# Linear attention and two gated layers on one core: both heads' numerators and denominators as products of 64 columns, normalised whole, in the first three blocks

## The chip, the cores and the metric

The kernel runs on one core of a Trainium2 chip. The metric is the device time of one execution in microseconds. The core has TensorE (PE, with its weight loads shown apart as PEld), VectorE (DVE), ScalarE (ACT), GpSimd (POOL) and SyncE (SP), whose queue here issues all DMAs. Each engine works off its own instructions in order and waits for the others by semaphores.

## The reference

Linear attention by random features for 4 x 8 heads of 576 tokens and 64 channels, then a gated layer, then a second layer. What the change touches is the end of the attention, `num` and `den`:

```python
q_p, k_p = phi(q_s), phi(k_s)                 # 128 features
kv = einsum('bhsm,bhsd->bhmd', k_p, v)
z = sum(k_p, axis=2)
num = einsum('bhsm,bhmd->bhsd', q_p, kv)
den = einsum('bhsm,bhm->bhs', q_p, z)[..., None] + 1e-06
x = num / den                                 # 2304 tokens x 512
g = x @ w_gate
x = (g / (1 + exp(-g)) * (x @ w_val)) @ w_out # 512 -> 1536 -> 512
h = x @ w_in                                  # 512 -> 2048
out = where(h >= 1, h, where(h <= -1, 0, (h + 1)**2 / 4)) @ w_out2
```

## The kernel before

The 2304 tokens are nine blocks of 256 (`k` = 0 to 8; a batch has 2.25 of them). The channels of a block lie in four pairs of heads (`p` = 0 to 3), and `d = p // 2` names the half of the 512 channels to which a pair belongs. Keys and values of a batch come in nine groups of 128 tokens (`k_group`): load `ki`, squares on ACT (L572), projection on PE (L599), maximum on DVE (L618), exponential on ACT into `ebk` (L626, or a DVE addition L630 and then L633), and products with the values `vi` (L672), which add up kv and z in a bank of PSUM. `kv_evac` copies that bank to `kvr` as f32 for the first three blocks, and to `kvz` in two parts for the others. The constant `NATK = 3` is the number of blocks that use f32 for this.

Queries (`q_group`) go the same way as far as the exponential (`ebq`), are transposed on PE (L757) and copied to `qtn`. Then `num` does one pair of heads of one block, and that is what is changed, for `k < NATK`; it runs 12 times there. For head `a` of the pair it multiplies the 256 columns of `qtn` with a 128 x 128 matrix of `kvr` (`mm_nat`, L810). The result of head 0 has its numerator on partitions 0 to 63 and its denominator, 64 times the same row, on partitions 64 to 127; for head 1 it is the other way about. Block 2 lies across two batches, and each product of it is two, of 64 and of 192 columns. After that:

- the two denominators are evicted to the other half of `rec`, with 1e-6 added, on ACT (L828) or DVE (L830);
- DVE transposes `rec` by squares of 32 into `rect` (L835), takes the reciprocal of one column of each square (L836) and transposes it back, spread over the square (L838);
- the numerators are multiplied by it, each half by itself: on DVE (L843), or copied by ACT (L848) and multiplied whole on POOL (L850).

The result `os` is split into two parts `x1s` (L373, L383, L385), which the first layer's products take (L392 to L394: high by high, high by low, low by high), and stored to `x1d`. `q_done` tells the stream of keys that a half block is through: the fifth to ninth key group of batch 2 are loaded only after the second half of blocks 0 to 2, by the plan.

What stands where in a queue is set when the program is built. A planner (`Planner`) runs all these processes against a table of costs; each engine takes the ready operation of the best priority, and `pick` gives an operation to the engine that would be done with it first. So any other cost or number of operations gives all engines another order. The order then stands in the program, and on the chip the engines only wait for each other. Buffers come from rings (`Get`, `pl.put`); eight banks of PSUM are one of them. A load into a buffer waits until what was in it has been read, and SP issues in order, so that what stands behind such a load waits too.

Of the kernel before, what the change touches and what calls it, by code (L numbers as in the profile page):

```python
# [22 lines left out]
AF = mybir.ActivationFunctionType  # L23
ALU = mybir.AluOpType
AX = mybir.AxisListType
# [3 lines left out]
P = 128  # L29
TB = 256  # L30
# [10 lines left out]
ALT = 1.63  # L41
# [5 lines left out]
NATK = 3  # L47
# [216 lines left out]
def c_act(n, bias=False):  # L264
    return (115 + n) / 1200.0 + (0.05 if bias else 0.0)


def c_dve(n, psum=False, fast=False):
    return (66 + (n / 2 if fast else n)) / 960.0


def c_pool(n):
    return 0.11 + 0.00218 * n
# [7 lines left out]
def performer_moe_kernel(ctx: ExitStack, tc: tile.TileContext, qG, kG, om, ident,  # L281
                         w1, wo1, w2, wo2, out):
    nc = tc.nc
    pl = Planner()
# [4 lines left out]
    def bufs(pool, name, n, shape, dt=F32):  # L289
        return [pool.tile(shape, dt, tag=f"{name}{i}", name=f"{name}{i}") for i in range(n)]  # L290

    def ring(*a):
        return Ring(bufs(*a))
# [6 lines left out]
    bank = ring(psum, "bank", 8, [P, 512])  # L300
# [19 lines left out]
    att = att_cm.__enter__()  # L320
# [30 lines left out]
    kvr = {(b, d): att.tile([P, 2, 2, P], F32, name=f"kvr{b}_{d}") for b in nat_b for d in range(2)}  # L351
    qts0 = ring(att, "qtn", 3, [P, 2, TB])
    xhl = ring(att, "xhl", 2, [P, 2, 256], F32R)
    stat = ring(att, "st", 10, [P, 4, 4])
    rec = ring(att, "rec", 2, [P, TB])
    rect = ring(att, "rect", 1, [P, TB])
    qts = ring(att, "qt", N_QT, [P, 2, 2, TB], F32R)
    kvz = [[att.tile([P, 2, 2, 2, P], F32R, name=f"kvz{b}_{d}") for d in range(2)] for b in range(2)]
    ids = att.tile([P, P], F32, name="ids")
    omr = att.tile([P, 256], F32, name="omr")  # L360
    omh = att.tile([P, 256], F32R, name="omh")
    oml = att.tile([P, 256], F32R, name="oml")
# [2 lines left out]
    def dma(dst, src, nbytes):  # L365
        yield Op("SP", 0.06, lambda: nc.sync.dma_start(dst, src))  # L366
        yield Op("HW", 0.05, None)
        yield Op("DMA", nbytes / 330e3, None)
# [210 lines left out]
    def margin():  # L579
        if moe_on.done and SLACK_A:  # L580
            yield SLACK_A
# [158 lines left out]
    def q_group(k, p, qb):  # L740
# [23 lines left out]
        else:  # L764
# [6 lines left out]
            else:  # L771
# [3 lines left out]
                yield Op("POOL", c_pool(512), lambda: nc.gpsimd.tensor_tensor(out=lv, in0=e, in1=hv.bitcast(F32), op=ALU.subtract))  # L775
                back(ebufs[True], e)
        pl.spawn(num(k, p, q_t), pl.cur.prio - 0.05)

    def num(k, p, q_t):
        d, r = divmod(p, 2)  # L780
        yield x1_have[k]
        xs = x1_tile[k]
        cuts = []
        t0 = k * TB
        while t0 < (k + 1) * TB:
            b = t0 // 576
            t1 = min((b + 1) * 576, (k + 1) * TB)
            cuts.append((b, t0 - k * TB, t1 - k * TB))
            t0 = t1
        if k < NATK:  # L790
            for b in sorted({c[0] for c in cuts}):
                yield kv_ready[b, d]
        else:
            for b in sorted({c[0] for c in cuts}):
                yield kv_split[b, d]
        if (k, d) not in xd:
            xd[k, d] = Ev(), []
            xd[k, d][1].append((yield Get(osb)))
            pl.set(xd[k, d][0])
        yield xd[k, d][0]  # L800
        x = xd[k, d][1][0]
        xr = x[:, r * TB:(r + 1) * TB]
        rc = yield Get(rec)
        pb = yield Get(bank)
        ps = pb.rearrange("p (a t) -> p a t", a=2)

        def mm_nat():
            for a in range(2):
                for b, c0, c1 in cuts:
                    nc.tensor.matmul(ps[:, a, c0:c1], kvr[b, d][:, r, a], q_t[:, a, c0:c1], start=True, stop=True)  # L810

        def mm():
            for a in range(2):
                for b, c0, c1 in cuts:
                    kz = kvz[b % 2][d]
                    for l, h in ((0, 0), (0, 1), (1, 0)):
                        nc.tensor.matmul(ps[:, a, c0:c1], kz[:, l, r, a], q_t[:, h, a, c0:c1],  # L817
                                         start=(l == 0 and h == 0), stop=(l == 1), skip_group_check=True)
        yield from margin()
        if k < NATK:  # L820
            yield Op("PE", 0.86 if len(cuts) == 1 else 0.95, mm_nat)
        else:
            yield Op("PE", 6 * 0.109 if len(cuts) == 1 else 12 * 0.107, mm)
        pl.put(qts if k >= NATK else qts0, q_t)
        half0, half1 = slice(0, 64), slice(64, P)
        for a, (here, there) in enumerate(((half0, half1), (half1, half0))):
            if pl.pick(ACT=c_act(TB), DVE=c_dve(TB)) == "ACT":
                yield Op("ACT", c_act(TB), lambda: nc.scalar.activation(rc[here], ps[there, a], AF.Copy, bias=1e-6))  # L828
            else:
                yield Op("DVE", c_dve(TB), lambda: nc.vector.tensor_scalar(  # L830
                    out=rc[here], in0=ps[there, a], scalar1=1e-6, scalar2=None, op0=ALU.add))
        tt = yield Get(rect)
        st = yield Get(stat)
        rs = st.rearrange("p a b -> p (a b)")[:, 0:TB // 32]
        yield Op("DVE", c_dve(TB), lambda: nc.vector.transpose(out=tt, in_=rc))  # L835
        yield Op("DVE", 0.135, lambda: nc.vector.reciprocal(out=rs, in_=tt.rearrange("p (n c) -> p n c", c=32)[:, :, 0]))  # L836
        pl.put(rect, tt)
        yield Op("DVE", c_dve(TB), lambda: nc.vector.transpose(  # L838
            out=rc.rearrange("p (n c) -> p n c", c=32), in_=rs.unsqueeze(2).to_broadcast([P, TB // 32, 32])))
        pl.put(stat, st)  # L840
        if pl.pick(DVE=2 * c_dve(TB), POOL=c_pool(TB) + 2 * c_act(TB) + ALT) == "DVE":
            for a, here in enumerate((half0, half1)):
                yield Op("DVE", c_dve(TB), lambda: nc.vector.tensor_tensor(  # L843
                    out=xr[here], in0=ps[here, a], in1=rc[here], op=ALU.mult))
            pl.put(bank, pb)
        else:
            for a, here in enumerate((half0, half1)):
                yield Op("ACT", c_act(TB), lambda: nc.scalar.activation(xr[here], ps[here, a], AF.Copy))  # L848
            pl.put(bank, pb)
            yield Op("POOL", c_pool(TB), lambda: nc.gpsimd.tensor_tensor(out=xr, in0=xr, in1=rc, op=ALU.mult))  # L850
        pl.put(rec, rc)
        q_cnt[k, d] = q_cnt.get((k, d), 0) + 1
        if q_cnt[k, d] < 2:
            return
        pl.set(q_done[k, d])
        yield from x1_split(k, d, x)
        yield from dma(half_block(x1d, k, d), x.rearrange("p (n t) -> p n t", n=2), P * 512 * 4)
        pl.put(osb, x)
# [4 lines left out]
    def half_block(t, k, d):  # L863

        return t[k // 2][:, 2 * d:2 * d + 2, (k % 2) * TB:(k % 2 + 1) * TB]

    def x1_split(k, d, x):
        xs = x1_tile[k]
        hi, lo = (xs[:, l, 2 * d:2 * d + 2].rearrange("p k t -> p (k t)") for l in range(2))
        yield from parts(hi, lo, x, 512)  # L870
        x1_cnt[k] = x1_cnt.get(k, 0) + 1
        if x1_cnt[k] == 2:
            pl.set(x1_ready[k])
# [347 lines left out]
    for m, a, order, sets in passes:  # L1221
        for j in order:
            for c in sets:
                n = 2 if m == 1 and j < 4 else 1 if m == 1 else 4 if j < 4 else 2
# [411 lines left out]
```

## Time and profile before

| | us |
|---|---|
| three timed runs, median (lowest, highest) | 993.88 (991.18, 995.39) |
| the profiled execution | 990.77 |
| its span, first to last instruction | 989.0 |
| PE busy | 968.7 |
| DVE busy | 830.2 |
| ACT busy | 573.8 |
| POOL busy | 100.4 |
| mean granted clock of PE, of 1 | 0.997 |

The profiled execution has its own time, 990.77 us; 1.8 us of it lie around the span. Busy times of a stretch are read against its length. A wait is idle time of an engine just ahead of an instruction, put down to whichever other engine or DMA came last. Matmul records overlap, so one takes longer than the time from one to the next. An f32 product is two instructions in the trace.

### The profile page before, as it was taken

To read this page: it belongs to the slowest core of one execution; us is meant where nothing else is said; L and a number is where in the kernel's file an instruction comes from. 1 tells how busy PE (TensorE), PEld (TensorE's weight loads), DVE (VectorE), ACT (ScalarE), POOL (GpSimd) and SP (SyncE) were. 2 spreads that over 40 slices of the span, in tenths; PEclk is the share of its full clock that TensorE was granted. 3 is DMA by queue.
4 is the path that set the end of the run, shared out by engine and by line. 5 is a ranking of instruction groups with operands and counts; after the bars stand their busy time and mean duration, and the time that the engine had idled before them with its cause. 6 is when DMAs were issued, how large, how long until landed. Compare 5 with 4: busy or idle time off the path is not lost.

```text
span 989.0 us, 18507 instructions
## 1 busy us (share of the span) xinstructions
PE 968.7 (98%) x6778; PEld 900.7 (91%) x6778; DVE 830.2 (84%) x1703; ACT 573.8 (58%) x1477; POOL 100.4 (10%) x101
## 2 busy tenths in 40 slices
PE   7899999999999999999999999999999999999998
PEld 6789899999999999999999999999998989999986
DVE  7999888778789999999999999998788678866553
ACT  8998888968654644464645556564555455544331
POOL 0223344733310000000000000000000000000000
PEclk9999999999999999999999999999999999999999
DMA  8755546545386555756575666246233041403022
GB/s 304 233 175 190 173 150 201 173 150 171 107 267 207 176 180 166 242 192 211 181 245 184 196 222 222 72 132 234 79 114 107 1 139 44 129 2 106 1 86 85
DMA packets 90667, 154.50 MB, mean 156 GB/s; under 512 B 8528, under 2 KB 42320, under 8 KB 90576
## 3 DMA queue, kind: packets, MB, share of 16 engines
q1 hardware_dynamic: 90576, 153.32, 47.6%
q8 instruction: 53, 0.87, 0.3%
q14 instruction: 38, 0.31, 0.1%
HBM read 110.30 MB, written 42.99 MB: 155 GB/s over the span
## 4 chain that ended last, share of the span: by engine, by line
PE 73%; DVE 11%; ACT 6%; DMA 5%; issue 3%; SPq 1%; POOL 0%; POOLq 0%; DVEq 0%; ACTq 0%
PE bank L392 22%; PE bank L394 22%; PE bank L393 22%; PE bank L672 2%; PE bank L599 2%; PE bank L817 1%; SPq L366 1%; PE bank L757 1%; DMA ws<-in_w_dram 1%; DMA ki<-in_kG_dram 1%; ACT ebq L626 1%; PE bank L810 1%; DVE wt L414 1%; DVE x1s L385 1%; ACT rec L828 1%
## 5 line engine op out<-in xcount | busy, mean ns | idle before, releaser
L392 PE MATMUL bank<-x1s,w 128*128 128x256 f32 x492 | 140.1, 285 | 2.7 <-ACT ebk L626 1.9
L394 PE MATMUL bank<-x1s,w 128*128 128x256 f32 x492 | 137.7, 280 | 0.0
L393 PE MATMUL bank<-x1s,w 128*128 128x256 f32 x492 | 137.6, 280 | 0.0
L392 PEld LDWEIGHTS bank<-x1s,w 128*128 128x128 f32 x492 | 92.7, 188 | 7.6 <-ACT ebk L626 2.3
L393 PEld LDWEIGHTS bank<-x1s,w 128*128 128x128 f32 x492 | 92.7, 188 | 3.8
L394 PEld LDWEIGHTS bank<-x1s,w 128*128 128x128 f32 x492 | 92.6, 188 | 0.0
L373 ACT ACTIVATE x1s<-xq 128x512 fp32r<-128x512 f32 x83 | 52.0, 628 | 51.3 <-PE bank L394 33.2
L392 PE MATMUL bank<-x1s,wb 128*128 128x256 f32 x286 | 80.1, 280 | 0.6 <-ACT eb L373 0.6
L394 PE MATMUL bank<-x1s,wb 128*128 128x256 f32 x286 | 79.9, 279 | 0.0
L393 PE MATMUL bank<-x1s,wb 128*128 128x256 f32 x286 | 79.9, 279 | 0.0
L392 PE MATMUL bank<-x1s,wx 128*128 128x256 f32 x278 | 78.7, 283 | 0.1
L394 PE MATMUL bank<-x1s,wx 128*128 128x256 f32 x278 | 78.4, 282 | 0.3 <-POOL wx L383 0.3
L393 PE MATMUL bank<-x1s,wx 128*128 128x256 f32 x278 | 78.4, 282 | 0.0
L373 ACT ACTIVATE eb<-bank 128x512 f32<-128x512 f32 x93 | 55.0, 592 | 28.7 <-PE bank L394 28.1
L385 DVE TENSOR_TENSOR x1s<-xq,x1s 128x512 fp32r<-128x512 f32 x90 | 61.5, 684 | 6.0 <-ACT x1s L373 5.9
L409 ACT ACTIVATE wt<-ws 128x512 f32<-128x512 f32 x68 | 45.7, 674 | 29.3 <-DMA ws<-in_wo_dram 14.9
L392 PEld LDWEIGHTS bank<-x1s,wb 128*128 128x128 f32 x286 | 54.0, 189 | 5.2 <-ACT eb L373 0.8
L393 PEld LDWEIGHTS bank<-x1s,wb 128*128 128x128 f32 x286 | 53.8, 188 | 4.3
L392 PEld LDWEIGHTS bank<-x1s,wx 128*128 128x128 f32 x278 | 52.6, 189 | 3.8 <-ACT eb L373 0.3
L393 PEld LDWEIGHTS bank<-x1s,wx 128*128 128x128 f32 x278 | 52.7, 190 | 3.3
L1251 DVE TENSOR_TENSOR gb<-bank,eb 128x512 f32<-128x512 f32 x64 | 43.8, 685 | 13.4 <-PE bank L394 13.2
L373 ACT ACTIVATE hlr<-hb 128x512 fp32r<-128x512 f32 x51 | 32.1, 630 | 38.7 <-PE bank L393 32.2
(267 smaller groups left out, 3205.7 us busy)
## 6 DMA issues: line engine op xcount, KB each, us to landing
ws<-in_w_dram SPq DMA_DIRECT2D x40, 512.0 KB, 4.9
ws<-in_wo_dram SPq DMA_DIRECT2D x28, 512.0 KB, 4.5
xq<-x1d SPq DMA_DIRECT2D x36, 256.0 KB, 5.0
xq<-x2d SPq DMA_DIRECT2D x36, 256.0 KB, 4.1
qi<-in_qG_dram SPq DMA_DIRECT2D x34, 256.0 KB, 3.1
ki<-in_kG_dram SPq DMA_DIRECT2D x33, 256.0 KB, 4.2
vi<-in_kG_dram SPq DMA_DIRECT2D x28, 192.0 KB, 3.3
x1d<-os SPq DMA_DIRECT2D x18, 256.0 KB, 3.7
```

Source lines behind the costliest of these rows:

```text
L366: yield Op("SP", 0.06, lambda: nc.sync.dma_start(dst, src))
L373: yield Op("ACT", c_act(n), lambda: nc.scalar.activation(dst, src, AF.Copy, scale=1.0 if scale is None else scale))
L385: yield Op("DVE", c_dve(n), lambda: nc.vector.tensor_tensor(out=dst, in0=a, in1=b, op=op), True)
L392: nc.tensor.matmul(ps, l_hi, r_hi, start=first, stop=False, skip_group_check=shared)
L393: nc.tensor.matmul(ps, l_hi, r_lo, start=False, stop=False, skip_group_check=shared)
L394: nc.tensor.matmul(ps, l_lo, r_hi, start=False, stop=last, skip_group_check=shared)
L409: yield Op("ACT", 0.575, lambda: nc.scalar.activation(t, hw.bitcast(F32), AF.Abs))
L414: yield Op("DVE", c_dve(512), lambda: nc.vector.scalar_tensor_tensor(out=ti, in0=lw, scalar=29, in1=ti, op0=ALU.logical_shift_right, op1=A ...
L599: nc.tensor.matmul(ps[:, t * 256:(t + 1) * 256], xt[:, t * P:(t + 1) * P], omr, start=True, stop=True)
L626: nc.scalar.activation(e[:, u * P:(u + 1) * P], ps[:, u * P:(u + 1) * P], AF.Exp, bias=st[:, u, 3:4])
L672: nc.tensor.matmul(kp[:, 2 * pr + a], e[:, u * P:(u + 1) * P], vb[:, vi + (dv if li == 4 else 0), a * 64:a * 64 + P], start=(li == 0 and a ...
L1251: yield Op("DVE", c_dve(512), lambda: nc.vector.tensor_tensor(out=dst, in0=pq(ps), in1=pq(e), op=ALU.add))
```

## The change

For blocks 0 to 2, each head's numerator and denominator are two products of 64 columns of `kvr`. Both numerators go to the same columns of PSUM (`ps[:, 0]`), head 0 on partitions 0 to 63 and head 1 on 64 to 127, and both denominators to `ps[:, 1]` in the same places. So denominators lie where their numerators lie, and the eviction to the other half falls away: DVE transposes the denominators right out of PSUM. `rect` gets a 33rd column for each square that holds 1e-6, and a reduction adds it to the denominator. The product with the reciprocal, or the copy for POOL, is one of 128 partitions instead of two of 64. The other six blocks do what they did (`norm_halves` has the old code). The plan's cost of `mm_nat` is left as it was.

```diff
-    rect = ring(att, "rect", 1, [P, TB])
+    rect = ring(att, "rect", 1, [P, TB // 32, 33])
+    nc.gpsimd.memset(rect.free[0][0][:, :, 32:33], 1e-6)
...
+    halves = slice(0, 64), slice(64, P)
+
+    def norm_whole(ps, pb, rc, xr):
+
+        tt = yield Get(rect)
+        st = yield Get(stat)
+        s8 = st.rearrange("p a b -> p (a b)")
+        yield Op("DVE", 0.36, lambda: nc.vector.transpose(out=tt[:, :, 0:32], in_=ps[:, 1].rearrange("p (n c) -> p n c", c=32)))
+        yield Op("DVE", 0.09, lambda: nc.vector.tensor_reduce(out=s8[:, 0:8], in_=tt[:, :, 0:33:32], axis=AX.X, op=ALU.add))
+        pl.put(rect, tt)
+        yield Op("DVE", 0.135, lambda: nc.vector.reciprocal(out=s8[:, 8:16], in_=s8[:, 0:8]))
+        yield Op("DVE", c_dve(TB), lambda: nc.vector.transpose(
+            out=rc.rearrange("p (n c) -> p n c", c=32), in_=s8[:, 8:16].unsqueeze(2).to_broadcast([P, TB // 32, 32])))
+        pl.put(stat, st)
+        if pl.pick(DVE=c_dve(TB), POOL=c_pool(TB) + c_act(TB) + ALT) == "DVE":
+            yield Op("DVE", c_dve(TB), lambda: nc.vector.tensor_tensor(out=xr, in0=ps[:, 0], in1=rc, op=ALU.mult))
+            pl.put(bank, pb)
+        else:
+            yield Op("ACT", c_act(TB), lambda: nc.scalar.activation(xr, ps[:, 0], AF.Copy))
+            pl.put(bank, pb)
+            yield Op("POOL", c_pool(TB), lambda: nc.gpsimd.tensor_tensor(out=xr, in0=xr, in1=rc, op=ALU.mult))
...
         def mm_nat():
-            for a in range(2):
+            for what in range(2):
                 for b, c0, c1 in cuts:
-                    nc.tensor.matmul(ps[:, a, c0:c1], kvr[b, d][:, r, a], q_t[:, a, c0:c1], start=True, stop=True)
+                    for a in range(2):
+                        nc.tensor.matmul(ps[halves[a], what, c0:c1], kvr[b, d][:, r, a, halves[a ^ what]], q_t[:, a, c0:c1],
+                                         start=True, stop=True, skip_group_check=True)
...
+        if k < NATK:
+            yield from norm_whole(ps, pb, rc, xr)
         else:
...
+            yield from norm_halves(ps, pb, rc, xr)
```

Since the plan is made anew, the order of all engines differs from about the first unit of `num` on. Two places. The first is on ACT, around the seventh exponential of queries (into `ebq_125`), for which PE's transposition at 44.31 us waits. `L828` (after: gone here) evicts a denominator, `L848` and `L798` copy numerators, `L572` and `L573` are squares. Before:

```order
L626 ACTIVATE ebq_126<-bank_67,st_158 128x128 x4
L373 ACTIVATE x1s_103<-os_111 128x512
L828 ACTIVATE rec_167<-bank_64 64x256
L828 ACTIVATE rec_166<-bank_69 64x256
L575 ACTIVATE qi_135<-qi_135 128x256
L572 ACTIVATE ki_127,st_163<-ki_127 128x64 x4
L373 ACTIVATE qtn_151<-bank_67 128x512
L572 ACTIVATE ki_128,st_157<-ki_128 128x64 x4
L848 ACTIVATE os_113<-bank_64 64x256
L633 ACTIVATE ebq_125<-ebq_125 128x512
L848 ACTIVATE os_113<-bank_64 64x256
```

The same place on ACT after:

```order
L374 ACTIVATE qtn_151<-bank_70 128x512
L627 ACTIVATE ebk_121<-bank_63,st_160 128x128 x4
L634 ACTIVATE ebk_124<-ebk_124 128x512
L573 ACTIVATE ki_127,st_163<-ki_127 128x64 x4
L573 ACTIVATE ki_128,st_165<-ki_128 128x64 x4
L798 ACTIVATE os_112<-bank_67 128x256
L576 ACTIVATE qi_135<-qi_135 128x256
L576 ACTIVATE ki_129<-ki_129 128x256
L410 ACTIVATE wt_83<-ws_81 128x512
L798 ACTIVATE os_112<-bank_64 128x256
L627 ACTIVATE ebq_125<-bank_68,st_164 128x128 x4
```

The evictions are gone, each copy is one instead of two, and two exponentials of keys (`ebk_121`, `ebk_124`) have moved ahead of this one of queries.

The second place is on PE, where batch 2's fifth key group is projected (`ki_128`, then `ki_129` and `ki_127`). The rows that are left out repeat the three products above them. Before:

```order
L672 MATMUL bank_65<-vi_130,ebk_123 128x128 x6
L392 MATMUL bank_64<-x1s_104,w_78 128x256
L393 MATMUL bank_64<-x1s_104,w_78 128x256
L394 MATMUL bank_64<-x1s_104,w_78 128x256
...
L672 MATMUL bank_65<-vi_131,ebk_124 128x128 x4
L599 MATMUL bank_67<-omr,ki_128 128x256 x2
```

After:

```order
L673 MATMUL bank_64<-vi_130,ebk_123 128x128 x2
L393 MATMUL bank_63<-hl_109,w_75 128x256
L394 MATMUL bank_63<-hl_109,w_75 128x256
L395 MATMUL bank_63<-hl_109,w_75 128x256
L673 MATMUL bank_64<-vi_131,ebk_124 128x128 x2
...
L395 MATMUL bank_65<-x1s_104,w_78 128x256
L600 MATMUL bank_67<-omr,ki_128 128x256 x2
```

Between the last read of `vi_130` and the projection stood 12 products of the layer and one row of `vi_131`; now 42 products of the layers and two rows of `vi_131` stand there. On SP the order at this place is the same in both: the load of `vi_130`, then the loads of `ki_128`, `ki_129` and `ki_127`.

## Rows read from the trace of the kernel before

**Rows 1.** Page, part 1: busy us (share of the span) and instructions of each engine.

```profile
PE 968.7 (98%) x6778; PEld 900.7 (91%) x6778; DVE 830.2 (84%) x1703; ACT 573.8 (58%) x1477; POOL 100.4 (10%) x101
```

**Rows 2.** Stretches: us, busy of each engine (instructions), granted clock, DMA share, GB/s.

```profile
30.00:40.00 10.00, 9.45 (x59) 8.36 (x59) 9.24 (x29) 9.86 (x38) 3.85 (x4) 1.00 0.83 271
40.00:50.00 10.00, 7.01 (x27) 4.81 (x25) 8.58 (x29) 9.29 (x46) 3.43 (x4) 0.83 0.63 194
50.00:60.00 10.00, 9.11 (x63) 8.35 (x64) 9.68 (x31) 9.93 (x40) 3.28 (x3) 1.00 0.55 165
...
100.00:110.00 10.00, 7.97 (x61) 7.29 (x60) 8.75 (x20) 7.55 (x28) 4.46 (x3) 0.98 0.68 200
110.00:120.00 10.00, 9.67 (x61) 8.76 (x60) 7.59 (x21) 8.17 (x38) 2.07 (x2) 0.85 0.60 206
...
sum 40.00, PE 36.95 PEld 36.14 DVE 32.40 ACT 36.23 POOL 20.91; mean PE 9.24 PEld 9.03 DVE 8.10 ACT 9.06 POOL 5.23
...
200.00:300.00 100.00, 99.98 (x854) 99.78 (x853) 81.22 (x173) 63.23 (x173) 29.74 (x27) 1.00 0.52 172
```

**Rows 3.** PE in order of time, 38 to 47 us: start, length, instructions, idle before.

```profile
38.46 1.13 PE L810 MATMUL bank<-qtn,kvr 128*128 128x256 f32 x4 [0.55 <-ACT kvr L373]
...
42.33 1.13 PE L599 MATMUL bank<-omr,qi 128*128 128x256 f32 x4 [1.43 <-DVE ebq L630]
44.31 0.67 PE L757 MATMUL bank<-ids,ebq 128*128 128x128 f32 x4 [0.86 <-ACT ebq L633]
44.80 1.92 PE L599 MATMUL bank<-omr,qi 128*128 128x256 f32 x4
```

**Rows 4.** ACT in order of time, 43 to 44.3 us.

```profile
43.37 0.37 ACT L848 ACTIVATE os<-bank 64x256 f32<-64x256 f32 x1
43.64 0.62 ACT L633 ACTIVATE ebq<-ebq 128x512 f32<-128x512 f32 x1
```

**Rows 5.** PE in order of time, 101 to 113 us.

```profile
101.47 2.39 PE L672 MATMUL bank<-vi,ebk 128*128 128x128 f32 x20
...
104.36 0.28 PE L394 MATMUL bank<-x1s,w 128*128 128x256 f32 x1
...
105.17 1.05 PE L672 MATMUL bank<-vi,ebk 128*128 128x128 f32 x8
108.15 4.64 PE L599 MATMUL bank<-omr,ki 128*128 128x256 f32 x12 [1.92 <-DMA ki<-in_kG_dram]
```

**Rows 6.** SP's queue in order of time, 102 to 106 us.

```profile
102.55 1.22 SPq L366 DMA_DIRECT2D vi<-in_kG_dram  x2
103.83 1.37 SPq L366 DMA_DIRECT2D ki<-in_kG_dram  x3
```

**Rows 7.** ACT's groups by form, 25 to 110 us: busy us, mean ns, idle before.

```profile
L828 ACT ACTIVATE rec<-bank 64x256 f32<-64x256 f32 x17 | 6.2, 377 | 0.9 <-PE bank L810 0.5
L848 ACT ACTIVATE os<-bank 64x256 f32<-64x256 f32 x10 | 3.7, 374 | 0.1
L575 ACT ACTIVATE ki<-ki 128x256 f32<-128x256 f32 x5 | 2.1, 428 | 0.0
```

**Rows 8.** PE in order of time at 36 us; PEld's group of L810, 0 to 200 us.

```profile
36.02 1.03 PE L599 MATMUL bank<-omr,ki 128*128 128x256 f32 x4
36.89 1.03 PE L810 MATMUL bank<-qtn,kvr 128*128 128x256 f32 x4
...
L810 PEld LDWEIGHTS bank<-qtn,kvr 128*128 128x128 f32 x64 | 10.7, 201 | 2.2 <-ACT kvr L373 1.0 <-ACT qtn L373 0.4
```

**Rows 9.** DVE's groups by form, 25 to 110 us.

```profile
L621 DVE TENSOR_REDUCE st<-st 128x4 f32<-128x8 f32 x53 | 6.5, 146 | 0.2
L843 DVE TENSOR_TENSOR os<-bank,rec 64x256 f32<-64x256 f32 x14 | 5.8, 411 | 0.2
L835 DVE STREAM_TRANSPOSE rect<-rec 128x256 f32<-128x256 f32 x12 | 5.1, 429 | 0.1
L830 DVE TENSOR_SCALAR rec<-bank 64x256 f32<-64x256 f32 x7 | 2.8, 417 | 1.2 <-ACT rec L828 1.0
```

More of the change, by code (lines that the diff above doesn't have):

```diff
@@ new lines, in norm_halves @@
+    def norm_halves(ps, pb, rc, xr):
+        for a, (here, there) in enumerate(((halves[0], halves[1]), (halves[1], halves[0]))):
+            if pl.pick(ACT=c_act(TB), DVE=c_dve(TB)) == "ACT":
+                yield Op("ACT", c_act(TB), lambda: nc.scalar.activation(rc[here], ps[there, a], AF.Copy, bias=1e-6))
+            else:
+                yield Op("DVE", c_dve(TB), lambda: nc.vector.tensor_scalar(
+                    out=rc[here], in0=ps[there, a], scalar1=1e-6, scalar2=None, op0=ALU.add))
+        tt = yield Get(rect)
+        st = yield Get(stat)
+        rs = st.rearrange("p a b -> p (a b)")[:, 0:TB // 32]
+        yield Op("DVE", c_dve(TB), lambda: nc.vector.transpose(out=tt[:, :, 0:32], in_=rc.rearrange("p (n c) -> p n c", c=32)))
+        yield Op("DVE", 0.135, lambda: nc.vector.reciprocal(out=rs, in_=tt[:, :, 0]))
+        pl.put(rect, tt)
+        yield Op("DVE", c_dve(TB), lambda: nc.vector.transpose(
+            out=rc.rearrange("p (n c) -> p n c", c=32), in_=rs.unsqueeze(2).to_broadcast([P, TB // 32, 32])))
+        pl.put(stat, st)
+        if pl.pick(DVE=2 * c_dve(TB), POOL=c_pool(TB) + 2 * c_act(TB) + ALT) == "DVE":
+            for a, here in enumerate((halves[0], halves[1])):
+                yield Op("DVE", c_dve(TB), lambda: nc.vector.tensor_tensor(
+                    out=xr[here], in0=ps[here, a], in1=rc[here], op=ALU.mult))
+            pl.put(bank, pb)
+        else:
+            for a, here in enumerate((halves[0], halves[1])):
+                yield Op("ACT", c_act(TB), lambda: nc.scalar.activation(xr[here], ps[here, a], AF.Copy))
+            pl.put(bank, pb)
+            yield Op("POOL", c_pool(TB), lambda: nc.gpsimd.tensor_tensor(out=xr, in0=xr, in1=rc, op=ALU.mult))
@@ L824, in num @@
         pl.put(qts if k >= NATK else qts0, q_t)
[L825 to L845, printed above, removed]
-        else:
[L847 to L850, printed above, removed]
+        if k < NATK:
+            yield from norm_whole(ps, pb, rc, xr)
+        else:
+            yield from norm_halves(ps, pb, rc, xr)
         pl.put(rec, rc)
```

## The prediction

> **What bounds the kernel now.** I read the busy times of the page first, then the stretches of 10 us, then in the stretches with idle TensorE its own order of time, and behind each of its waits the engine that was waited for. The page has PE busy for 968.7 of 989.0 us [rows 1]. The stretches say where the other 20 us are: from 200 us on PE is full (99.98 of 100 us in the stretch shown), so the change cannot save anything there, it can only disturb. The idle time lies ahead of that, and the three blocks that the change touches are worked on between 27 and 105 us. In 30 to 60 us PE is idle for 0.55 + 2.99 + 0.89 = 4.43 us, and in the middle one of these stretches the granted clock has a mean of 0.83; in 100 to 120 us it is idle for 2.03 + 0.33 = 2.36 us, with clocks of 0.98 and 0.85; in 150 to 190 us for 40.00 - 36.95 = 3.05 us [rows 2].
>
> The first idle stretch is made by ACT and DVE, which are busy for 9.86 + 9.29 + 9.93 = 29.1 us and 27.5 us of these 30 [rows 2]. PE waits 1.43 us until DVE's addition ebq L630 and 0.86 us until ACT's exponential ebq L633 [rows 3]. That exponential stands on ACT right behind a copy of a half (os L848 [rows 4]), and the order shows two evictions of denominators (rec L828) and the next half's copy around it. After those two waits four instructions at 44.80 take 1.92 us where the same four take 1.03 us elsewhere [rows 3, 8]: PE had been idle, and the granted clock then stood at 1.2 of 2.4 GHz. Time lost by it: 10 us x 0.17 = 1.7 us.
>
> The second one is a DMA: PE waits 1.92 us for ki at 108.15, and then twelve instructions take 4.64 us, again at half the clock; (0.02 + 0.15) x 10 = 1.7 us are lost by that [rows 2, 5]. Those loads were issued at 103.83, right behind two loads of vi in SP's queue [rows 6]. The second of these (into vi_130) may not start before PE has read the old vi_130, with the last twelve of the twenty instructions that start at 101.47 and last 2.39 us [rows 5].
>
> **The change, part by part.** *DVE and ACT.* In each of the 12 units (3 blocks x 4 pairs of heads; "unit" below) two evictions of 64 x 256 fall away, 17 on ACT of 377 ns and 7 on DVE of 417 ns, together 9.3 us; and two half products (or half copies) become one whole of the same 256 columns, which saves 12 instructions of 374 to 411 ns, 4.7 us [rows 7, 9]. That a whole one costs what a half does: 128x256 on ACT takes 428 ns, 64x256 takes 374 to 377 [rows 7]. Added is one small reduction for each unit, nearest row 146 ns, 1.8 us in all [rows 9]. The transpose now reads PSUM and writes at a pitch of 33; the nearest row is its old form with 429 ns, and the row of a product that reads 256 columns from PSUM has 411 [rows 9]. I take 0.43 and no change; if the pitch doubled it, that would be 12 x 0.43 = 5.2 us more on DVE, less than what is taken off. Net: 12.2 us less on the two engines, about 7 of the 12 units before 60 us, so 7 us out of that stretch's 56.6.
>
> *PE's first idle stretch.* The order shows what this moves. On ACT, two evictions and the half copies no longer stand ahead of the exponential of ebq_125. I added up the work that the orders put ahead of each transposition on ACT and on PE, each instruction by what rows of its kind take (an estimate): before, ACT's sum is ahead of PE's by 1.8, 3.2 and 2.0 us for the three transpositions around 42 us, so PE must wait; in the new order ACT's is less than PE's by 1.6 to 5.9 us from the fifth to the fourteenth, so PE need not. I count the idle 4.43 us as gone but for the 0.55 us for kvr at 38.46, which has the same neighbours in the new order [rows 3]; and as PE does not idle, the 1.7 us of slow clock go with it. -5.6 us.
>
> *PE's second one.* In SP's queue the loads of ki still stand behind vi_130. But between the last read of the old vi_130 and the first use of ki, PE's new order has 42 products of 0.117 us (104.36 to 105.17 for seven) and 4 of 0.22 us: 5.8 us; before, there were 12 and 4, 2.3 us [rows 5]. From their issue to their first use the loads took 103.83 to 108.15, 4.3 us [rows 5, 6]. So 3.5 us of cover are added where 1.92 were missing: the wait goes, and the slow clock behind it. -3.6 us. What is late next there is nothing that I can name from the rows; the idle 0.33 us and 0.1 us are left.
>
> *PE's third one.* Which waits of 150 to 190 us survive a new order I can't tell: ACT is ahead by more at nearly all places there. Between nothing and 3.05 us I take half, -1.5 us.
>
> *PE's own work.* A unit was 2 products of 256 columns in f32, 4 instructions, 0.87 us (36.02 to 36.89 for four such [rows 8]). Now it is 4 products of 64 output columns, 8 instructions, that still pass all 256 columns each. The trace has no product that fills half the array, so this is bounded: if two products on different halves run side by side all the time, 0.87 us, nothing added; if one after another, 8 x 0.216 = 1.73 us, 12 x 0.86 = 10.4 us more. The code alternates the halves, but each product is two instructions in a row on the same half; if only neighbours on different halves pair, 8 instructions take 5 slots of 0.216, 1.08 us. I take this value, 12 x 0.21 = +2.5 us: it is nearest to the lower end, because PE's rows show that it takes up an instruction before the last is through (a record of 1.03 us for four that come every 0.87 [rows 8]), but it is the least certain term here. After 60 us nothing hides it.
>
> The Trainium skill (TensorEngine Tiling (Array Packing), Key Properties) says that tiles operate independently and can load and multiply in parallel; no run here shows that yet. By it alone the term would be between 0 and +2.5 us. The same section says that a change of the tiling mode drains the engine; there are 24 such changes, and no row prices one.
>
> *Sum.* 990.8 us (989.0 of span and 1.8 around it) - 5.6 - 3.6 - 1.5 + 2.5 = 982.6 us. The profiled run was the fastest seen: the median of the three timed ones is 993.9 and they spread over 4.2 us. Against the median the same difference of -8.2 us gives 985.7; I forecast 986.
>
> **The rivals.** *One after another.* The halves don't pair: +10.4 instead of +2.5. The idle time still goes, since a slower PE waits less: 993.9 - 10.7 + 10.4 = 993.6, no change that can be told. For it: no row of the trace shows two products side by side. Against it: the halves lie on different partitions and are written in turn. Chance 0.25.
>
> *Weights in the open* (slower than before). Each of the 8 instructions of a unit loads its 64 columns, and the load can't hide behind a product that uses the same rows of the array. The price from the rows: at least the pace of 128-column instructions, 0.11 us (105.17 to 106.03 for eight [rows 5]), at most the record of a load, 0.20 us [rows 8]. With 0.11 a unit is 8 x 0.326 = 2.6 us, +20.9 us in all: 993.9 - 10.7 + 20.9 = 1004. It decides from 0.87 + 10.7/12 = 1.76 us a unit, and by more than 0.5% from 2.17. Against it: now the loads do hide, as four instructions with loads of 0.20 us come every 0.87 us. Chance 0.10.
> The Trainium skill (TensorE: Matmul & The Clock Gate, Part 3) has the rule that a load overlaps products in flight only when the row group differs, and here both halves use all rows. The trace disagrees for whole-array products, whose loads overlap.
>
> *The holes move.* All queues are planned anew, and PE's idle time comes back elsewhere ahead of 200 us, with its slow clock: 993.9 + 2.5 = 996.4 at worst, 992 if half of it does. For it: the three holes of before have three different causes. Against it: the sums on ACT above are better everywhere. Chance 0.15.
>
> **How the numbers follow.** The forecast has 0.50. Within it the third idle stretch (0 to 3) and the pairing (0 to 2.5) leave 982 to 990. A measurement of this kernel can tell 0.5%, 5 us, from no change. Faster by more: most of the forecast's 0.50 and a few lucky cases of the others, 0.48. Within 0.5%: the rest of the forecast, one after another, most of the moved holes, 0.38. Slower: the weights in the open and the worst of the holes, 0.14. The range goes from 980 (all holes gone, full pairing) to 997 (holes come back).
>
> **What would show it.** Right: PE busy for nearly all of 30 to 60 us, no granted clock below 1 there or in 100 to 120 us, no wait for ki near 105; units of 1.1 us in PE's order of time. Wrong: a unit of 1.7 us or more, with PE full and the span unchanged; or PE's waits for ebq, ki or a bank back under other names. The forecast fails first at the unit's price on PE.

## The result and the profile after

The kernel after takes 984.08 us (median of four runs, 983.49 to 984.53), the kernel before 994.63 in the same comparison (991.18 to 995.78): ratio 0.9896, with a 95% interval of 0.9874 to 0.9917. 986.0 was forecast. The profiled execution of after took 984.11 us with a span of 982.1; that of before had 990.77 and 989.0.

Page, part 1, of the kernel after: busy us (share of the span) and instructions. [rows 1] answers to it.

```profile
PE 966.7 (98%) x6842; PEld 895.3 (91%) x6842; DVE 825.7 (84%) x1697; ACT 567.3 (58%) x1459; POOL 107.7 (11%) x110
```

The stretches of the kernel after; the columns are those of [rows 2]: us, then busy time of PE, PEld, DVE, ACT and POOL with their instructions, granted clock, DMA share, GB/s.

```profile
30.00:40.00 10.00, 10.00 (x74) 8.39 (x73) 9.57 (x32) 9.90 (x38) 5.23 (x5) 1.00 0.91 288
40.00:50.00 10.00, 10.00 (x72) 8.13 (x71) 9.19 (x38) 8.72 (x41) 4.69 (x5) 1.00 0.87 283
50.00:60.00 10.00, 9.72 (x69) 7.53 (x69) 8.46 (x29) 8.00 (x35) 2.12 (x3) 1.00 0.40 108
100.00:110.00 10.00, 8.74 (x57) 7.68 (x55) 8.49 (x25) 8.25 (x40) 2.64 (x2) 1.00 0.71 236
110.00:120.00 10.00, 9.97 (x86) 9.97 (x87) 8.33 (x20) 8.38 (x22) 5.62 (x6) 1.00 0.42 127
150.00:190.00 40.00, 40.00 (x345) 40.00 (x344) 34.95 (x90) 37.19 (x156) 28.67 (x31) 1.00 0.63 197
300.00:500.00 200.00, 197.40 (x1431) 185.38 (x1430) 190.03 (x365) 105.66 (x196) 0.00 (x0) 1.00 0.61 199
...
980.00:982.00 2.00, 0.00 (x0) 0.00 (x0) 0.00 (x0) 0.00 (x0) 0.00 (x0) 0.77 0.13 44
```

Of the first two holes that the prediction named, that of 30 to 60 us is closed but for 0.28 us; in 100 to 120 us 1.29 of 2.36 us are left, behind other waits. No clock below 1 is left in either. The idle time of PE, from such rows over the whole span, in both profiled executions and in a second one of before that was taken later (last of the experiments):

| stretch, us | idle before | idle before, second profile | idle after |
|---|---|---|---|
| 0 to 20 | 5.38 | 4.78 | 5.24 |
| 30 to 60 | 4.43 | 4.86 | 0.28 |
| 60 to 100 | 0.25 | 0.26 | 0 |
| 100 to 120 | 2.36 | 3.80 | 1.29 |
| 120 to 200 | 3.05 | 3.18 | 0.75 |
| 200 to 700 | 0.95 | 4.45 | 2.60 |
| 700 to the end | 3.87 | 3.86 | 5.27 |
| sum | 20.3 | 25.2 | 15.4 |

So 4.9 us of idle time are gone against the first profile of before. Slow clock, reckoned as stretch x (1 - granted clock), cost 3.4 us before (1.7 + 0.2 + 1.5, [rows 2]) and nothing after: the one fall there, at 981 us, comes when PE has run its last instruction. PE is busy for 966.7 us after; before it was 968.7 us, without the 3.4 us 965.3. Its own work became 1.4 us dearer. -4.9 - 3.4 + 1.4 = -6.9 us: that is the difference of the spans. Against the second profile of before it is 11.8 us, of which 9.8 are idle time; the difference of the medians, 10.6 us, lies between the two.

TensorE in order of time in the kernel after: start, length, instructions, idle before. L862 are the new products (L810 before).

```profile
26.79 1.50 PE L673 MATMUL bank<-vi,el 128*128 128x128 f32 x12
28.22 1.95 PE L862 MATMUL bank<-qtn,kvr 128*64 128x256 f32 x16
30.10 0.66 PE L758 MATMUL bank<-ids,ebq 128*128 128x128 f32 x4
...
31.04 1.03 PE L600 MATMUL bank<-omr,qi 128*128 128x256 f32 x4
...
44.55 1.08 PE L862 MATMUL bank<-qtn,kvr 128*64 128x256 f32 x8
45.56 1.13 PE L600 MATMUL bank<-omr,ki 128*128 128x256 f32 x4
...
63.76 1.10 PE L862 MATMUL bank<-qtn,kvr 128*64 128x64 f32 x16
64.79 1.13 PE L600 MATMUL bank<-omr,qi 128*128 128x256 f32 x4
...
89.03 1.99 PE L862 MATMUL bank<-qtn,kvr 128*64 128x64 f32 x32
90.94 0.66 PE L758 MATMUL bank<-ids,ebq 128*128 128x128 f32 x4
...
101.10 2.75 PE L600 MATMUL bank<-omr,ki 128*128 128x256 f32 x12
...
105.70 1.10 PE L600 MATMUL bank<-omr,ki 128*128 128x256 f32 x4 [0.45 <-DMA ki<-in_kG_dram]
```

From start to the next start, one unit alone takes 1.01 us (44.55 to 45.56), two in a row 1.88 (28.22 to 30.10): the second unit costs 0.87, as much as a unit of before [rows 8], and 0.14 to 0.15 us come on top once for each group (units that follow each other on PE without anything between). Block 2, with 16 short instructions a unit, reads the same: 1.03 for one, 1.91 for two.

A group also delays its neighbours. TensorE in order of time in the kernel before, first the same instructions as at 26.79 to 31.04 above, then two units of block 2:

```profile
26.32 1.50 PE L672 MATMUL bank<-vi,el 128*128 128x128 f32 x12
27.65 1.89 PE L810 MATMUL bank<-qtn,kvr 128*128 128x256 f32 x8
...
30.27 1.03 PE L599 MATMUL bank<-omr,qi 128*128 128x256 f32 x4
...
74.21 2.36 PE L810 MATMUL bank<-qtn,kvr 128*128 128x64 f32 x16
76.40 0.60 PE L757 MATMUL bank<-ids,ebq 128*128 128x128 f32 x4
```

From the product of vi to the projection of qi it was 3.95 us (26.32 to 30.27) and is 4.25 (26.79 to 31.04): a group costs 0.30 us, 0.10 ahead of it (1.43 instead of 1.33 us from the product of vi to the group), 0.15 in it and 0.05 behind it.

The 8 units of blocks 0 and 1 stand in six groups: 6 x 0.30 = +1.8 us. Block 2 was dearer before: two units took 2.19 us and take 1.91 - 0.15 = 1.76 now but for the group's share, 0.22 less for each, so that its four units in three groups come to 3 x 0.30 - 4 x 0.22 = 0. This count gives +1.8 us, the busy time above +1.4.

SP's queue in the kernel after, where the loads of ki for 101.10 are issued [rows 6]:

```profile
95.48 0.42 SPq L367 DMA_DIRECT2D vi<-in_kG_dram  x1
95.95 1.38 SPq L367 DMA_DIRECT2D ki<-in_kG_dram  x3
```

They still stand right behind a load of vi, but their first use comes 5.15 us after the issue (101.10 - 95.95), without a wait and at the full clock: 2.75 us for what took 4.64 [rows 5].

DVE's groups by form, 25 to 110 us, in the kernel after [rows 9]:

```profile
L787 DVE STREAM_TRANSPOSE rect<-bank 128x256 f32<-128x256 f32 x12 | 5.2, 430 | 0.7 <-PE bank L862 0.6
L788 DVE TENSOR_REDUCE st<-rect 128x8 f32<-128x16 f32 x12 | 1.9, 156 | 0.0
L795 DVE TENSOR_TENSOR os<-bank,rec 128x256 f32<-128x256 f32 x4 | 1.7, 413 | 0.0
```

And ACT's, where the copies of whole pairs stand [rows 7]:

```profile
L798 ACT ACTIVATE os<-bank 128x256 f32<-128x256 f32 x8 | 3.2, 399 | 0.0
```

The transposition out of PSUM takes 430 ns where the old one took 429, the reduction 156, and an operation of 128 partitions about what one of 64 took (413 against 411 ns on DVE, 399 against 374 on ACT).

### The profile page after: what moved, and what is told of

It is laid out like the page before. It is cut to its first block, busy times and chain, and to the rows that moved or that the text cites. A ratio compares the mean times of both kernels' runs of the same rounds, so it can differ in the third digit from the quotient of the medians.

```text
span 982.1 us, 18629 instructions
## 1 busy us (share of the span) xinstructions
PE 966.7 (98%) x6842; PEld 895.3 (91%) x6842; DVE 825.7 (84%) x1697; ACT 567.3 (58%) x1459; POOL 107.7 (11%) x110
## 4 chain that ended last, share of the span: by engine, by line
PE 84%; DVE 6%; DMA 5%; ACT 2%; issue 1%; SPq 1%; POOL 0%; DVEq 0%; POOLq 0%; ACTq 0%
PE bank L393 25%; PE bank L395 25%; PE bank L394 25%; PE bank L673 3%; PE bank L600 3%; DMA xq<-x1d 2%; PE bank L870 2%; PE bank L758 1%; PE bank L862 1%; DMA wtr<-w32g 1%; DMA ki<-in_kG_dram 1%; DMA ws<-in_w_dram 1%; DMA kl<-in_kG_dram 1%; SPq L367 1%; DVE st L619 0%
## 5 line engine op out<-in xcount | busy, mean ns | idle before, releaser
L374 ACT ACTIVATE hl<-hb 128x512 fp32r<-128x512 f32 x63 | 39.7, 630 | 53.0 <-PE bank L394 38.7
L386 DVE TENSOR_TENSOR hl<-hb,hl 128x512 fp32r<-128x512 f32 x57 | 39.4, 691 | 23.5 <-ACT hl L374 21.0
L393 PEld LDWEIGHTS bank<-x1s,wx 128*128 128x128 f32 x278 | 52.6, 189 | 5.9 <-ACT eb L374 2.1
L619 DVE TENSOR_REDUCE st<-bank 128x4 f32<-128x512 f32 x72 | 48.3, 682 | 10.1 <-PE bank L395 5.6
```

The source lines that it names most:

```text
L374: yield Op("ACT", c_act(n), lambda: nc.scalar.activation(dst, src, AF.Copy, scale=1.0 if scale is None else scale))
L386: yield Op("DVE", c_dve(n), lambda: nc.vector.tensor_tensor(out=dst, in0=a, in1=b, op=op), True)
L393: nc.tensor.matmul(ps, l_hi, r_hi, start=first, stop=False, skip_group_check=shared)
L619: yield Op("DVE", c_dve(512), lambda: nc.vector.tensor_reduce(out=st[:, :, 0], in_=psv, axis=AX.X, op=ALU.max, negate=True))
```

## The experiments

Three things change at once: the products on PE, the work of DVE and ACT, and the order on all engines. The runs take them apart. The last two columns are read from each run's profile: PE's idle time and what slow clock cost.

| kernel | median, us | ratio to before, interval | idle + slow clock 30 to 60 us | 100 to 120 us |
|---|---|---|---|---|
| before, first profile | | | 4.4 + 1.7 | 2.4 + 1.7 |
| before, second profile | 992.14 | 0.9996 (0.9976 to 1.0016) | 4.9 + 0 | 3.8 + 1.7 |
| new products alone | 993.53 | 1.0007 (0.9991 to 1.0024) | 4.8 + 0 | 3.4 + 0 |
| old work, ki first | 989.12 | 0.9968 (0.995 to 0.9986) | 4.1 + 1.7 | 1.7 + 0 |
| old work, planned anew | 989.19 | 0.9963 (0.994 to 0.9986) | 5.2 + 0 | 0.3 + 0 |
| old work in after's order | 998.03 | 1.0054 (1.0034 to 1.0074) | 7.0 + 1.2 | 2.5 + 0 |
| new work in before's order | 988.07 | 0.9964 (0.9944 to 0.9983) | 2.1 + 0 | 2.9 + 0 |
| the same, ki first | 986.9 | 0.9945 (0.9917 to 0.9973) | 2.7 + 0 | 1.1 + 0 |
| after, planned anew | 984.07 | 0.9904 (0.9877 to 0.993) | 2.6 + 1.7 | 0.6 + 0 |
| after, ki first | 984.24 | 0.9913 (0.9888 to 0.9937) | 0.1 + 0 | 2.2 + 1.7 |
| after | 984.08 | 0.9896 (0.9874 to 0.9917) | 0.3 + 0 | 1.3 + 0 |

**New products alone.** The kernel before with 64-column products in the places of the old, all else as it was:

```diff
-                    nc.tensor.matmul(ps[:, a, c0:c1], kvr[b, d][:, r, a], q_t[:, a, c0:c1], start=True, stop=True)
+                    for h in (slice(0, 64), slice(64, P)):
+                        nc.tensor.matmul(ps[h, a, c0:c1], kvr[b, d][:, r, a, h], q_t[:, a, c0:c1],
+                                         start=True, stop=True, skip_group_check=True)
```

> The kernel before, with only PE's part of the change: each product of 128 columns as two of 64 on the two halves, in turn, into the same places of PSUM as before; the normalisation and every queue's order are those of before. In the changed kernel a unit took 0.94 to 1.02 us on PE instead of 0.87. Theory (the halves pair, and the gain comes from ACT and DVE): 12 x 0.1 = +1.2 us, so between 994 and 997 with the holes of before at 40 to 50 and 100 to 112 us. Rival (the new products themselves are what gains): 990 or less. Rival (they only pair in the new arrangement): a unit of 1.73 us, up to +10 us, 1000 to 1005.

993.53 us, no change. TensorE in order of time:

```profile
26.32 1.50 PE L672 MATMUL bank<-vi,el 128*128 128x128 f32 x12
27.75 1.95 PE L811 MATMUL bank<-qtn,kvr 128*64 128x256 f32 x16
...
30.57 1.03 PE L599 MATMUL bank<-omr,qi 128*128 128x256 f32 x4
```

With every order as before, the same instructions take 4.25 us here as well (26.32 to 30.57), 0.30 more than with whole products. In the time of the kernel PE's part of the change neither gains nor costs anything that can be told.

**New work in before's order.** The new products, transposition and whole products, but every step is put where the old one stood; the evictions' places in the plan are kept and left empty:

```diff
+                yield Op("ACT", c_act(TB), old(lambda: nc.scalar.activation(rc[here], ps[there, a], AF.Copy, bias=1e-6)))
...
+            out=tt[:, :, 0:32], in_=(ps[:, 1] if new else rc).rearrange("p (n c) -> p n c", c=32)))
```

> The whole of the new work (products of 64 columns, no evictions, one whole product with the reciprocal), but written in the order that the plan of before gave: what is left out leaves its place empty. Theory A (less work on ACT and DVE closes the first hole, the order of the loads closes the second): first hole gone, -5.6 us, second still there, units +1.2 us: 990 (988 to 992). Theory B (it is the new order of all queues that gains): still 994 to 996. Theory C (less work closes both holes): 986.

988.07 us, ratio 0.9964. Part 1 of its page and its stretches:

```profile
PE 965.6 (98%) x6842; PEld 895.5 (91%) x6842; DVE 827.3 (84%) x1701; ACT 564.9 (57%) x1455; POOL 99.8 (10%) x102
...
40.00:50.00 10.00, 7.86 (x52) 5.76 (x51) 9.74 (x34) 9.56 (x45) 2.43 (x4) 1.00 0.52 169
...
150.00:190.00 40.00, 37.40 (x319) 37.20 (x319) 32.20 (x87) 36.17 (x147) 24.90 (x29) 1.00 0.58 186
```

And its waits on PE, 25 to 120 us (in total, times, longest):

```profile
PE bank L758 <- ACT ebq L634: 2.0, 2, 1.3
PE bank L600 <- DMA ki<-in_kG_dram: 1.6, 1, 1.6
```

The relief of ACT and DVE alone halves the first hole, but the exponential ebq is still late in the old order, and the wait for ki (1.6 us) and the idle time of 150 to 190 us (2.6) stay.

**Old work in after's order.** Every engine has after's order, with the 24 evictions and the half products put back into it, which this order wasn't planned for. In three of the twelve units of these two kernels the denominators are transposed before they are evicted (in the second at 50.80, 66.14 and 103.30 us, the evictions begin at 51.77, 66.84 and 103.82): there a wait is left out that the old work needs. The amount of work is that of before. The second has the reciprocal one place earlier.

```diff
...
+            for a in range(2):
+                pl.push(pl.now + 1.2, evict, ps, rc, a)
...
```

> The changed kernel's order of all queues, with the old work put back into it: products of 128 columns, 24 evictions (17 on ACT, 7 on DVE) that the plan doesn't know of, and two half products instead of one whole. Theory A: the holes at 30 to 60 us come back at least in part, 12.2 us more on ACT and DVE against 1.2 us less on PE: 987 to 991. Theory B (order alone): 983 to 985.

> The changed kernel's order of all queues with the old work put back into it (products of 128 columns, 24 evictions that the plan doesn't know of, half products), as in the run before it, now with the reciprocal read before its buffer is given back. Theory A (less work on ACT and DVE is needed for the new order to be full): the holes come back, 988 or more; the run before it had 999. Theory B (order alone): 983 to 985.

999.38 us (ratio 1.0064, 1.004 to 1.0088) and 998.03 us (1.0054): slower than before. Waits on PE of the second, 25 to 120 us (in total, times, longest), and a stretch of it:

```profile
PE bank L393 <- ACT qtn L374: 3.1, 1, 3.1
PE bank L600 <- DMA ki<-in_kG_dram: 2.5, 1, 2.5
PE bank L877 <- ACT kvr L374: 2.3, 1, 2.3
...
150.00:190.00 40.00, 39.70 (x341) 39.50 (x340) 34.88 (x98) 34.91 (x143) 21.77 (x23) 1.00 0.61 193
```

ACT is what two of the three longest waits are for. After's order isn't good in itself; with the old work in it the first hole is larger than ever (7.0 us). That the gain comes from the order alone falls.

**Not in turn.** The kernel after with all products of head 0 (half 0) ahead of all of head 1:

```diff
-            for what in range(2):
-                for b, c0, c1 in cuts:
-                    for a in range(2):
+            for a in range(2):
+                for what in range(2):
+                    for b, c0, c1 in cuts:
```

> The changed kernel, with the four products of a unit not in turn on the two halves but head 0's two first and then head 1's; order of everything else as in the changed kernel. Theory (neighbours on different halves overlap): only one pair of neighbours is left in each unit, so a unit goes from 0.95 to about 1.5 to 1.7 us, 12 x 0.65 = +8 us, 990 to 993. Rival (64 columns cost half as much on PE by themselves): no change, 984.

985.4 us, ratio 0.9925 (0.9899 to 0.995); the interval overlaps that of after. My expectation of a loss was wrong. TensorE in order of time:

```profile
43.67 1.09 PE L862 MATMUL bank<-qtn,kvr 128*64 128x256 f32 x8
44.70 1.13 PE L600 MATMUL bank<-omr,ki 128*128 128x256 f32 x4
...
62.38 1.60 PE L862 MATMUL bank<-qtn,kvr 128*64 128x64 f32 x16
63.90 1.13 PE L600 MATMUL bank<-omr,qi 128*128 128x256 f32 x4
```

With 8 instructions the unit takes 1.03 us, in turn 1.01; with 16 short ones 1.52 against 1.03. So it isn't only neighbours that run side by side: four instructions on one half leave room for the four behind them, eight short ones leave less.

**Four more products on one half.** The kernel after with four more products a unit, all on half 0, which write the same values again:

```diff
+            for what in (0, 1, 0, 1):
+                for b, c0, c1 in cuts:
+                    nc.tensor.matmul(ps[halves[0], what, c0:c1], kvr[b, d][:, r, 0, halves[what]], q_t[:, 0, c0:c1],
+                                     start=True, stop=True, skip_group_check=True)
```

> The changed kernel, with four more products in each unit, all on half 0 (they write the same values once more), so 8 more instructions on one half in a row. Theory P (a product of 64 columns takes 0.216 us for each of its instructions, and two halves run side by side): +8 x 0.216 = 1.7 us a unit, +21 us, about 1005. Theory Q (an instruction of an f32 product with 64 columns takes half of one with 128, wherever it is): +8 x 0.11 = 0.9 us a unit, +11 us, about 995.

1003.07 us in one execution. TensorE in order of time (L866 are the added ones):

```profile
54.94 1.08 PE L862 MATMUL bank<-qtn,kvr 128*64 128x256 f32 x8
55.85 1.89 PE L866 MATMUL bank<-qtn,kvr 128*64 128x256 f32 x8
57.68 0.66 PE L758 MATMUL bank<-ids,ebq 128*128 128x128 f32 x4
```

Eight instructions on two halves take 0.91 us, eight on one 1.83 us. An instruction of 64 columns is not cheaper than one of 128 (0.87 / 4 = 0.22 us [rows 8]; 1.83 / 8 = 0.23): the halves run side by side.

**ki first.** The kernel before, and then the one with new work in before's order, with three loads of ki ahead of two of vi in SP's queue:

```diff
...
+        yield Op("SP", 0.06, (lambda: later.append(load)) if (b, g) in ((2, 6), (2, 7)) else load)
...
```

> The kernel before, all work and all orders as they were, except that on SP the three loads of ki for batch 2's fifth to seventh key group are issued ahead of the two loads of vi that they stood behind. Theory (the hole at 106 us is these loads waiting behind vi, and the slow clock follows from it): -1.9 us of wait and up to -1.7 us of slow clock, against about 992.7: 989 to 991. Rival (another wait takes its place): 992 to 994.

> The new work in the order of before (988.1 in its own run), and ki ahead of vi as well. Theory (the two causes add, and together they are the gain): 984 to 986, as the changed kernel. Rival (the rest of the gain is the new order elsewhere, after 120 us): 987 to 988.

989.12 us (0.9968) and 986.9 us (0.9945). The first one's SP queue in order of time, where [rows 6] has the two the other way about:

```profile
98.12 1.37 SPq L647 DMA_DIRECT2D ki<-in_kG_dram  x3
101.82 1.22 SPq L710 DMA_DIRECT2D vi<-in_kG_dram  x2
```

And PE there, with no wait and at the full clock:

```profile
105.34 2.76 PE L599 MATMUL bank<-omr,ki 128*128 128x256 f32 x12
```

So the wait behind vi is the cause of the second hole, and freeing the loads is worth 992.51 - 989.12 = 3.4 us with the old work. The second kernel, with both edits, has 992.51 - 986.9 = 5.6 us, against 4.6 for the new work alone (992.70 - 988.07); the intervals overlap, so that these two add up is not shown.

**Planned anew.** The plan's cost of the products, 0.86 and 0.95 us, set to 0.95 and 1.03, in before and in after: the work stays, all orders change.

```diff
-            yield Op("PE", 0.86 if len(cuts) == 1 else 0.95, mm_nat)
+            yield Op("PE", 0.95 if len(cuts) == 1 else 1.03, mm_nat)
```

> The kernel before with nothing changed but the plan's cost of the products on PE (0.86 and 0.95 us become 0.95 and 1.03), so that all queues are planned anew; the work is that of before. Theory W (the gain of the change is work taken off DVE and ACT, and an order of K loads that this re-planning need not give): the idle stretches of 30 to 60 and 100 to 120 us stay, though perhaps elsewhere in them; 990 to 996 us, ratio to before 0.998 to 1.003. Theory L (luck of the plan: any new plan of so many queues may give or take 5 us, and the gain of the change is of that kind): the time may come out anywhere between 985 and 1000; a ratio under 0.995 would speak for L.

> The kernel after with the same edit of the plan's cost, 0.95 and 1.03 us (which is about what a unit takes there on the chip), so the same new work in one more order. Theory W: PE stays busy in 30 to 60 us, since the work taken off DVE and ACT doesn't depend on the order; 982 to 988 us, ratio to before 0.988 to 0.995. Theory L: the idle time of 100 to 120 us, which hangs on the place of the K loads in SP's queue, and that of 300 to 500 us come out differently each time; 984 to 993 us, overlapping with before replanned.

Before planned anew takes 989.19 us (0.9963): faster than I expected of it from the work theory. Its stretches:

```profile
40.00:50.00 10.00, 6.59 (x31) 4.74 (x30) 9.62 (x32) 9.85 (x41) 3.96 (x5) 1.00 0.65 199
...
100.00:110.00 10.00, 10.00 (x81) 9.78 (x80) 9.71 (x21) 8.88 (x39) 2.90 (x2) 1.00 0.78 245
```

The first hole is still there (5.2 us in 30 to 60), the second is gone: closing it takes no new work, only another order. After planned anew takes 984.07 us, as after does, though its first hole is back in part (2.6 us) and the clock fell behind it:

```profile
50.00:60.00 10.00, 10.00 (x63) 8.18 (x63) 6.92 (x21) 8.00 (x35) 2.75 (x3) 0.83 0.42 128
```

Neither theory holds by itself. A new plan alone was worth 3 us here; but the two intervals for re-planned kernels (0.994 to 0.9986 and 0.9877 to 0.993) don't meet, which speaks for the work being worth something on top. With one new plan of each kind it is not shown how far plans differ among themselves.

**After with ki first.** The same edit of SP's order in the kernel after.

> The kernel after with three loads of ki issued ahead of two of vi by SP, as in the run of before with that edit; all other orders are as after. If the place of these loads is why before lost 3.3 us there, after, which has only 0.45 us of that wait left at 105.70, gains 0.4 us at the most: 983 to 985 us, ratio to before 0.989 to 0.992. If instead the loads are the bound of that stretch in both kernels, it gains 1 to 2 us: 982 to 983.

984.24 us, no change: what was to be had there is had. In its profile the next load of ki is late in its place (2.2 us of idle time in 100 to 120), and the time is the same.

**Before once more.** The kernel before unchanged, for a second profile.

> The kernel before, unchanged, for a second profiled execution of it. Theory A (the 2.6 us that PE idles in 300 to 500 us in the kernel after were brought by the change): this execution has PE busy for 199.5 to 200 of 200 us there, as the first one, and the three holes before 200 us as in the first. Theory B (the first profiled execution, 990.77 us, was one of the luckier ones, and before idles there too in most): 197 to 199 of 200 us, and 992 to 995 us in time. The holes of 30 to 60 and 100 to 120 us are expected in both, 4 to 5 and 2 to 3 us of idle time.

The profiled execution took 995.69 us, with a span of 993.9. Its stretches:

```profile
40.00:50.00 10.00, 5.97 (x30) 4.38 (x31) 9.46 (x32) 9.82 (x48) 2.31 (x3) 1.00 0.52 153
...
110.00:120.00 10.00, 7.88 (x51) 7.54 (x50) 7.19 (x18) 7.62 (x28) 3.74 (x3) 0.83 0.43 140
...
300.00:500.00 200.00, 197.81 (x1453) 186.83 (x1453) 190.72 (x367) 100.01 (x185) 0.00 (x0) 1.00 0.59 196
```

The two holes are there again. In 300 to 500 us PE idles for 2.2 us, where the first profile had 0.1 and after has 2.6: that idle time was not brought by the change. All the other profiles, of old and new work, have 2.2 to 3.7 us there; the first profile of before is the exception.

## Why the prediction was right

**The first hole (-5.6 forecast).** 4.43 - 0.28 of idle time and 1.7 of slow clock are gone, 5.9 us. The cause was right: ACT and DVE were late. In the profiles with the old normalisation, whatever the order, PE idles for 4.1 to 7.0 us in 30 to 60; in those with the new one for 0 to 2.7. That all of it goes took the new order as well: in before's order half stayed. The slow clock was counted as certain behind a hole, and it isn't: the kernel with new products alone idles 4.6 us in 40 to 50 at a granted clock of 1.00, the second profile of before 4.0 us at 1.00, the first 3.0 us at 0.83. How much slow clock an execution has differs besides: it cost 1.4 to 3.4 us in the seven profiles with the old work, in three of them in part at 319, 379 and 619 us, where the change does nothing, and 0 to 3.0 us in the seven with the new. That all 3.4 us are gone in the profile of after is luck in part.

**The second hole (-3.6).** In the two profiles 1.07 of idle time and 1.7 of slow clock went, 2.8 us; the wait at the place in question went wholly, and 0.45 us for the next ki and 0.63 for another tile (xhl) came behind it. The cause, loads of ki held up behind vi, is shown by the run that turns only their order (-3.4 us). But the prediction booked the gain to the change as if it followed from it; it follows from the new order, which an edit of the plan's costs gives to the old work too.

**The third hole (-1.5).** All 3.05 us of 150 to 190 us went, and 0.75 came back in 120 to 150 and 190 to 200. Taking half was a guess, and -2.3 came out. In 150 to 190 us the new work in before's order leaves 2.6 us and the old work in after's order 0.3: by these two profiles this hole was closed by the order, not by the work.

**PE's own work (+2.5): near in size, by another mechanism.** It measured +1.4 us by the busy time and +1.8 counted group by group. What failed is "if only neighbours on different halves pair, 8 instructions take 5 slots". The halves run side by side throughout, so that a further unit takes 0.87 us, and what I had at the lower end was right for the unit itself; instead there are 0.30 us for each group of units, which I had left without a price, and block 2's short products became cheaper, which I had not seen since I took one unit's price for all. That the sum came near is luck. The Trainium skill (TensorEngine Tiling (Array Packing), Key Properties) says both, that tiles work independently and that a change of the tiling mode drains the engine. The 0.30 us at a group's borders fit the second; that they are this drain was not tested apart. The Trainium skill's rule that loads overlap only when the row group differs (TensorE: Matmul & The Clock Gate, Part 3), behind the rival of weights in the open, does not hold here: with it a unit was to take 2.6 us.

**DVE and ACT (-12.2 us of work).** The sizes held: 430 ns for the transposition (0.43), 156 for the reduction (146), 399 and 413 for whole operations. The run with the new work in before's order tests the sum: DVE has 2.9 and ACT 8.9 us less there than in the first profile of before, 11.8 together. In after it is 4.5 and 6.5 us, 11 together, and POOL has 7.3 more; but that holds something else too: the new plan moved five subtractions of split queries (into qt) from DVE to POOL, 6.9 us there, and gave POOL three more products with the reciprocal, 1.6 us.

**What was not foreseen.** After has 2.6 us of idle time in 300 to 500 and 1.4 us more at the end. The first is in before as well, in its second profile: "from 200 us on PE is full" held for the one execution that the prediction read. It took a better one than usual for the base, 990.8 against a median of 993.9, and by transferring only the difference to the median it did not suffer. The 1.4 us at the end are in the profiles of after and of the run not in turn (5.3 and 5.4 us); the other twelve, of old and new work, have 3.9. Its cause stays open.

**Rivals.** One after another (1.73 us a unit) would have looked like the row of the added products on one half, 1.83 us; it needed both heads to share a half. Weights in the open: no unit near 2.6 us. (Its 106.03 is in no row: the record of the eight ends at 106.22; they start 0.11 us apart, as it says.) The holes that move came true in part: 0.75 and 1.1 us of new waits, and before's order with the new work still has all three holes, the first by half. The new order alone was not among my rivals as a source of gain; it should have been, at 3 us.

**How much is work and how much order.** It does not split into two numbers. The new work is worth 0.36% in before's order (0.9964), and 1.6% in after's (1.0054 against 0.9896); the order is worth about 0.4% of gain or 0.5% of loss with the old work and 0.7% of gain with the new (0.9964 against 0.9896). What the runs show is that the new work in five other forms (four orders and one with products out of turn) stays between 0.9904 and 0.9964, and that no order tried with the old work came below 0.9963.

## What to carry to other kernels

Put two results that will be combined elementwise on the same partitions when the matmul that makes them can: the products on halves of the output took what whole ones did, here 0.87 us a unit, plus 0.30 us for each group, and two evictions a unit fall away. When a planner makes all queues anew, compare with the old work planned anew before you credit the work with the gain, and profile the base twice. Here an idle stretch of the bound engine that other engines made shrank by half when their work shrank, and closed with a plan made for the new work; one made by a load held up in a queue closed when the load moved, whatever the work.

## What the runs showed of the hardware

- Two 64-column f32 products on different halves take no longer than one of 128 columns: 8 instructions in 0.87 us, and 0.30 us for each group of them between whole-array products, at its borders. Eight in a row on one half take 1.83 us. They need not be strictly in turn: four and four still take 1.03 us (1.01 in turn), eight and eight short ones 1.52 instead of 1.03.
- A transposition by DVE that reads PSUM and writes with a pitch of 33 takes 430 ns, as from SBUF with a pitch of 32 (429).
- The granted clock behind a hole doesn't follow the hole's length: 1.00 in a stretch of 10 us with 4.6 us of idle time, 0.83 in one with 3.0.
- The executions of before spread over 987.65 to 998.67 us in one comparison of 13, those of after over 983.49 to 984.53 in four. It is not the new work alone that runs more evenly: in before's order it spreads over 986.86 to 993.88 us in ten. The cause stays open.
